# Two more tile pairs of block 0 by Strassen's identity, and statistics by way of DRAM, in a fused LayerNorm, state-space and feed-forward kernel

## The chip, the cores and the metric

One Trainium2 chip, one core. The time is device microseconds of one execution; the kernel before takes 357.88 us, the median of three runs (357.68 to 357.89). The engines are TensorE (PE, with its weight loads as PEld), VectorE (DVE), ScalarE (ACT), GpSimd (POOL) and SyncE (SP, which only issues transfers here).

## The reference

The input is u of [1, 2048, 640]. The output is the sum of three things: u itself, a state-space layer of the normalised u, and a feed-forward layer of the normalised u.

```
xn  = layernorm(u)                      # over the 640 features
K   = 2 Re sum_n C[d,n] exp(dt A[d,n])^l
ssm = causal_conv(xn, K) + xn * D_skip  # over the 2048 positions
h   = xn @ w1 + b1                      # 640 -> 1728
ffn = (h * tanh(softplus(h))) @ w2      # 1728 -> 640
out = u + ssm + ffn
```

## The kernel before, in words

Everything is held transposed, features on partitions: KD = 5 slabs of 128 features, and positions along the rows, in NB = 4 blocks of TB = 512. The hidden size is cut into 14 tiles (FC): tiles 0 to 7 and 9 to 13 have 128 units, tile 8 (HALF) has 64.

The feed-forward products are made in float16. Each operand is split in a high and a low part (xh and xl for x, w1h and w1l, w2h and w2l, hi and lo for the activations), and three products are added in PSUM: high by high, low by high, high by low. A tile of the first layer (mm1, L807) is therefore 5 slabs x 3 = 15 matmuls of 512 columns, and so is a tile of the second layer (mm2_ops, run at L859). The second layer follows LAG = 3 tiles behind.

Two tiles that lie side by side (PAIRS names the first: 0, 2, 4, 6, 9, 11) can be made together by Strassen's identity in Winograd's form (mm1_pair, L809 to L834). Four slabs of x and of w1 and the two halves of the block's positions form 2 x 2 blocks, of which 7 products are needed and not 8; the fifth slab is done plainly. That makes 54 matmuls of 256 columns in five pieces: one (12), two (15), three_a and three_b (9 each) and four (9). In between, ACT copies two partial results out of PSUM (cV and cY, L1049 and L1050) and DVE adds one to another (z, L1053, wanted by three_a; w, L1057, wanted by four). Pieces of second layers stand between the five, so that these steps have time. A pair needs more operands: sums and differences of the block's x (sum_x at L613, their high parts th at L616 and low parts tl at L620), once for a block, and sums of the two weight tiles (sum_w at L580 to L586, their high and low parts at L598 and L602), once for the kernel. In the kernel before, pairs are used in blocks 1 to 3; block 0 makes all its tiles plainly. The sums of the weights are made from tiles that are loaded a second time (load_s, L573).

After a first layer come the activation's steps: ACT's s (L890), DVE's A (L894), three ACT steps p (L898 to L906), DVE's A (L910), then hi (ACT, L916) and lo (DVE, L926).

LayerNorm. Block 0 is normalised in the start-up, position by position. Later blocks load u twice. Untransposed tiles x feed the statistics (st, DVE, L627 to L629; four for a block). POOL turns the variances into factors (rstds, L633, L634, L1213). The means and the factors, 128 x 8, are turned by a PE transpose (spread, L638), copied by ACT (L642), stored to DRAM as 8 rows (sd, L646) and broadcast to all partitions (bc, L650). Transposed slabs xt are loaded, and DVE subtracts the mean and multiplies by the factor (L654, both operations; ten for a block). Then xh and xl are made (L565, L568). 

The state-space layer. Parameters are checked to be so small that the convolution comes to prefix sums within given bounds; the checks and the few constants are DVE and ACT steps on parameter tiles (L671 to L690, and the exponentials at L197 to L212), called the preparation of the parameters below. The sums are the skip steps (L743 to L763). A value per partition, ok, gathers the checks of parameters and weights; a matmul with ones (ok_sum, L731) adds it over the partitions, DVE makes the flag of it, and every engine reads the flag (L734). If it is set, a general path runs behind. In block 0, x is put together again from xh and xl for these steps (x0_sum, L1197).

Joining. A block's second layer is copied out of PSUM (join, L768 on DVE for two slabs, L770 on ACT for three), u is added by a POOL transfer that accumulates (L548), the result is accumulated on the state-space part (L773), and stored.

The order of the work. PE's order is written out in whole(). For ACT, DVE, SP and POOL a planner (class Plan) goes along a model of the time and takes, on each engine, the ready step with the earliest due time; due times are worked out backwards from PE's. An engine then runs its steps in just this order: a step that waits holds up all behind it. So each number of cost, gap or due time moves steps.

## Time and profile before

| | us |
|---|---|
| median of three runs | 357.88 |
| span of the profiled execution | 356.0 |
| PE busy | 350.0 |
| DVE busy | 305.9 |
| ACT busy | 295.8 |
| POOL busy | 48.9 |
| block 0's pairable tiles 9 to 13 begin on PE | 57.9 |
| block 1 begins on PE | 88.8 |
| block 2 begins | 173.4 |
| block 3 begins | 258.0 |

The page's span is the time from the first to the last instruction of one profiled execution; the runs' time is 1.9 us longer than that. Matmuls overlap: a row's duration is longer than the time to the next row's start, and a price on PE is taken from start to start. Names in rows leave out buffer numbers; L859 is line 859 of the kernel before.

### The profile page before, as it was taken

Reading aid. Unit: us, or ns where it says so; the run is one execution under the profiler, and the core shown is the slowest. Engines: PE = TensorE matmul, PEld = TensorE weight load, DVE = VectorE, ACT = ScalarE, POOL = GpSimd, SP = SyncE. Lnnn points to the kernel's source line nnn. Section 1 sums busy time; section 2 is a strip of 40 time slices with the busy share of each in tenths; the row PEclk is TensorE's granted clock in tenths of the full one; section 3 lists DMA queues with packets and bytes.
Section 4 is the critical chain, followed back from the end, with each engine's and each line's share of the span. In section 5 each row is a group of like instructions: output and inputs, shape, how many; then the busy total and the mean of one; then the engine's idle time right before and its main releaser. Section 6 shows DMA issues by size and latency. Waiting matters only on the chain.

```text
span 356.0 us, 6197 instructions
## 1 busy us (share of the span) xinstructions
PE 350.0 (98%) x2257; PEld 215.1 (60%) x2257; DVE 305.9 (86%) x583; ACT 295.8 (83%) x620; POOL 48.9 (14%) x74
## 2 busy tenths in 40 slices
PE   7999999999999999999999999999999999999996
PEld 6754444444666666665566666566566666666543
DVE  5989989989999999999999877899988878895552
ACT  4699999987598699989899977989989979877650
POOL 2200010000014221000004341000002443000000
PEclk9999999999999999999999999999999999999999
DMA  7869964402819926910445982931000994032004
GB/s 266 327 175 288 321 217 121 142 0 66 287 56 159 295 71 142 347 40 3 130 151 88 252 204 77 309 120 40 28 0 7 164 216 102 18 58 32 2 2 152
DMA packets 26052, 48.75 MB, mean 137 GB/s; under 512 B 3592, under 2 KB 6944, under 8 KB 26016
## 3 DMA queue, kind: packets, MB, share of 16 engines
q1 hardware_dynamic: 19488, 34.86, 30.0%
q0 software_dynamic: 6240, 13.11, 18.5%
q8 instruction: 19, 0.31, 0.4%
q10 hardware_dynamic: 288, 0.33, 0.3%
q14 instruction: 17, 0.14, 0.2%
HBM read 39.10 MB, written 5.26 MB: 125 GB/s over the span
## 4 chain that ended last, share of the span: by engine, by line
PE 96%; DVE 1%; DMA 1%; ACT 0%; issue 0%
PE acc L859 48%; PE h L827 18%; PE h L807 12%; PE tr L827 12%; PE h L800 2%; PE h L789 2%; PE tr L789 1%; DMA x<-in_A_u_dram 1%; PE acc L1236 0%; DVE st L627 0%; DVE st L628 0%; ACT x L1224 0%; PE acc L873 0%; PE acc L871 0%; PE acc L870 0%; DVE w1l L556 0%
## 5 line engine op out<-in xcount | busy, mean ns | idle before, releaser
L859 PE MATMUL acc<-hi,w2h 128*128 128x512 f16 x273 | 100.9, 379 | 0.0
L859 PE MATMUL acc<-hi,w2l 128*128 128x512 f16 (+1 forms) x265 | 99.7, 379 | 0.0
L859 PE MATMUL acc<-lo,w2h 128*128 128x512 f16 x253 | 93.3, 379 | 0.0
L859 PEld LDWEIGHTS <-w2h 128*128 128x128 f16 x526 | 50.9, 98 | 48.3 <-issue 2.1
L890 ACT ACTIVATE s<-h,cv 128x512 f32<-128x512 f32 (+1 forms) x55 | 32.7, 595 | 28.6 <-PE h L827 23.4
L827 PEld LDWEIGHTS <-w1h 128*128 128x128 f16 x432 | 42.3, 98 | 10.7
L910 DVE SCALAR_TENSOR_TENSOR A<-p,A 128x512 f32<-128x512 f32 (+1 forms) x56 | 37.1, 662 | 8.5 <-ACT p L906 8.2
L859 PEld LDWEIGHTS <-w2l 128*128 128x128 f16 x273 | 25.6, 98 | 30.7 <-issue 1.1
L926 DVE SCALAR_TENSOR_TENSOR lo<-A,hi 128x512 f16<-128x512 f32 x52 | 35.5, 683 | 8.0 <-ACT hi L916 8.0
L894 DVE SCALAR_TENSOR_TENSOR A<-h,bs,s 128x512 f32<-128x512 f32 (+1 forms) x55 | 34.9, 637 | 6.2 <-ACT s L890 6.2
L898 ACT ACTIVATE p<-s,kc 128x512 f32<-128x512 f32 (+1 forms) x56 | 39.4, 703 | 0.6
L902 ACT ACTIVATE p<-p,kc 128x512 f32<-128x512 f32 (+1 forms) x56 | 39.4, 703 | 0.5
L906 ACT ACTIVATE p<-p,kc 128x512 f32<-128x512 f32 (+1 forms) x56 | 39.3, 702 | 0.4
L916 ACT ACTIVATE hi<-A 128x512 f16<-128x512 f32 x52 | 32.5, 626 | 2.6 <-DVE A L910 2.5
L548 POOL DMA_DIRECT2D r<-in_xT_dram x15 | 13.4, 1003 | 131.7 <-DVE r L768 66.3
L749 DVE TENSOR_TENSOR_SCAN g<-g,car,kc 128x512 f32<-128x512 f32 x20 | 25.6, 1278 | 1.7 <-ACT g L743 1.7
L827 PEld LDWEIGHTS <-w1l 128*128 128x128 f16 x216 | 21.1, 98 | 8.2
L753 DVE TENSOR_TENSOR_SCAN g<-g,car,g 128x512 f32<-128x512 f32 x20 | 25.5, 1276 | 0.0
L827 PE MATMUL tr<-xh,w1l 128*128 128x256 f16 x90 | 24.5, 273 | 0.0
L827 PE MATMUL tr<-xh,w1h 128*128 128x256 f16 x90 | 24.5, 273 | 0.0
L827 PE MATMUL tr<-xl,w1h 128*128 128x256 f16 x90 | 24.5, 273 | 0.0
L827 PEld LDWEIGHTS <-swh 128*128 128x128 f16 x216 | 21.1, 98 | 4.4
(177 smaller groups left out, 726.6 us busy)
## 6 DMA issues: line engine op xcount, KB each, us to landing
w<-in_w_dram SPq DMA_DIRECT2D x25, 320.0 KB, 4.9
x<-in_A_u_dram SPq DMA_DIRECT2D x14, 320.0 KB, 5.0
w<-in_w2T_dram SPq DMA_DIRECT2D x15, 288.0 KB, 6.4
w<-in_B_w_dram SPq DMA_DIRECT2D x13, 320.0 KB, 3.4
w<-in_w1T_dram SPq DMA_DIRECT2D x13, 320.0 KB, 7.0
xt<-in_xT_dram SPq DMA_DIRECT2D x15, 256.0 KB, 5.6
r<-in_xT_dram POOLq DMA_DIRECT2D x15, 256.0 KB, 5.6
xt<-r POOLq DMA_DIRECT2D x15, 256.0 KB, 4.6
```

Of the source, the lines that this page charges most:

```text
L749: v.tensor_tensor_scan(g1[:, 1:], g1[:, 1:], zero.to_broadcast([P, TB]), car[:, 1, k:k + 1], op0=OP.add, op1=OP.add)
L807: pe.matmul(o, w, x, start=(j == 0), stop=(j == len(order) - 1))
L827: pe.matmul(o, p, q, start=start and n == 1, stop=n == 3 * len(w), skip_group_check=True)
L859: pe.matmul(o, w, x, start=start, stop=stop)
L890: a.activation(pl["s", b, f][:, c], bank(b, f)[:, c] if h is None else h, AF.Sigmoid, bias=cv[:, f:f + 1], scale=1 / SH)
L894: v.scalar_tensor_tensor(pl["A", b, f][:, c], bank(b, f)[:, c] if h is None else h, bs[:, f:f + 1], pl["s", b, f][:, c], op0=OP.add, op1=O ...
L898: a.activation(pl["p", b, f][:, cols(f)], pl["s", b, f][:, cols(f)], AF.Arctan, bias=one, scale=-1.0)
L902: a.activation(p, p, AF.Square, bias=pi4, scale=2.0)
L906: a.activation(p, p, AF.Tanh, bias=mb, scale=MG)
L910: v.scalar_tensor_tensor(A, pl["p", b, f][:, cols(f)], MC, A, op0=OP.add, op1=OP.mult)
L916: a.activation(hi, A, AF.Copy, scale=MA * SA / SH)
L926: v.scalar_tensor_tensor(lo, A, MA * SA / SH, hi, op0=OP.mult, op1=OP.subtract)
```

## The change

Five things are changed, and the order of nearly all steps with them.

1. Block 0's tiles 9 and 10, 11 and 12 (EARLY) are made as pairs. For that, block 0's x sums with their high and low parts are made (sums(0, ...)), the x0 sums are made early, and these two pairs' weight sums come from the w1 tiles that lie in SBUF for block 0 anyhow (sum_w with own), so that their second loads go. Tiles 9 to 13 use the PSUM banks in the later blocks' way (bank).
2. The statistics are stored to DRAM straight from the partitions (spread_d: 128 partitions with 8 values each, to a [8, 128] array read as r p -> p r). The PE transpose and ACT's copy go. POOL stores the mean's negative.
3. The mean is no longer subtracted on DVE. Five POOL transfers for a block read the stored row, broadcast it and accumulate it on the loaded slab (center). DVE keeps the multiplication.
4. The flag: ok is stored to DRAM, read back as a row, and DVE takes its minimum; ok_sum's matmul goes.
5. All joins are on ACT. The preparation of the parameters is due in block 1, tile 7, and no longer at block 0's end; costs, gaps and other due times are new, and SHIFT moves single due times by a table of some 270 numbers.

How the order changes at the places that matter. First DVE in block 0, when PE works on tiles 9 and 10. Before, w2l, hi and A belong to the running tiles, par and mx to the preparation of the parameters:

```order
L674 TENSOR_REDUCE mx_463<-par_564 128x10
L926 SCALAR_TENSOR_TENSOR lo3_256<-A1_245,hi3_255 128x512 [waits Activation_49]
L678 SCALAR_TENSOR_TENSOR par_564,sm_464<-par_564,dt_110 128x128 [waits DVE_49]
L910 SCALAR_TENSOR_TENSOR A0_244<-p0_247,A0_244 128x256 [waits Activation_49]
L678 SCALAR_TENSOR_TENSOR par_564,sm_464<-par_564,dt_110 128x128
L580 TENSOR_TENSOR t0_229<-w6_225 128x256 [waits DMAHW7_49]
L678 SCALAR_TENSOR_TENSOR par_564,sm_464<-par_564,dt_110 128x128
L562 SCALAR_TENSOR_TENSOR w2l9_163<-w3_222,w2h9_149 128x640 [waits DMAHW0_49,Activation_49]
L678 SCALAR_TENSOR_TENSOR par_564,sm_464<-par_564,dt_110 128x128
L582 TENSOR_TENSOR t0_229<-t0_229,w1_220 128x256 [waits DMAHW6_49,DVE_49]
```
After, t2 with xt is an x difference, tl and el low parts of such, swl and w1l those of weight sums, st_905 the last of block 1's four statistics, and L1080 the first new pair's z:

```order
L638 SCALAR_TENSOR_TENSOR swl4_196<-t2_229,swh4_190 128x256
L638 SCALAR_TENSOR_TENSOR w1l12_136<-t0_227,w1h12_123 128x2x128 [waits Activation_49]
L649 TENSOR_TENSOR t2_229<-xt_643,t3_230 128x512 [waits DVE_49]
L656 SCALAR_TENSOR_TENSOR el_207<-t1_228,eh_206 128x256 [waits Activation_49]
L945 SCALAR_TENSOR_TENSOR A1_242<-p0_244,A1_242 128x512
L945 SCALAR_TENSOR_TENSOR A0_241<-p1_245,A0_241 128x256 [waits Activation_49]
L656 SCALAR_TENSOR_TENSOR tl3_205<-t2_229,th3_201 128x512 [waits Activation_49]
L961 SCALAR_TENSOR_TENSOR lo3_253<-A1_242,hi3_252 128x512 [waits Activation_49]
L663 BN_STATS st_905<-x1_226 128x6 [waits DMAHW6_49]
L664 BN_STATS st_905<-x1_226 128x6
L665 BN_AGGR mv_570<-st_905 128x2 [waits DVE_49]
L1080 TENSOR_TENSOR h0_209<-h1_210,pvs_211 128x256 [waits PE_49]
```
The preparation of the parameters is gone from here, sums and their low parts have come, and the statistics have moved back from far ahead to right before z.

Second DVE some 10 us later, where block 1 is normalised. Before, L654 is the subtraction (bc0) and the multiplication (bc1), among steps of the parameters:

```order
L654 TENSOR_TENSOR xt_575<-xt_575,bc0_240 128x512 [waits DMAHW1_49]
L910 SCALAR_TENSOR_TENSOR A2_246<-p1_248,A2_246 128x512 [waits DVE_49,Activation_49]
L678 SCALAR_TENSOR_TENSOR par_564,sm_464<-par_564,dt_110 128x128
L654 TENSOR_TENSOR xt_575<-xt_575,bc0_240 128x512
L678 SCALAR_TENSOR_TENSOR par_564,sm_464<-par_564,dt_110 128x128
L654 TENSOR_TENSOR xt_575<-xt_575,bc0_240 128x512
L926 SCALAR_TENSOR_TENSOR lo1_252<-A2_246,hi1_251 128x512 [waits PE_49,Activation_49]
L681 TENSOR_TENSOR mx_463<-mx_463 128x5
L654 TENSOR_TENSOR xt_575<-xt_575,bc0_240 128x512
L894 SCALAR_TENSOR_TENSOR A1_245<-h1_212,bs_104,s0_242 128x512 [waits Activation_49]
```
After, L1080 and L1084 are z and w of the second new pair, and L684 is the multiplication, which waits for the accumulating transfer of the mean (a DMASW semaphore):

```order
L945 SCALAR_TENSOR_TENSOR A1_242<-p1_245,A1_242 128x512 [waits Activation_49]
L1080 TENSOR_TENSOR h0_209<-h1_210,pvs_211 128x256 [waits PE_49]
L684 TENSOR_TENSOR xt_576<-xt_576,bc0_238 128x512 [waits DMAHW3_49,DMASW0_49]
L929 SCALAR_TENSOR_TENSOR A0_241<-tr_208,bs_102,s1_240 128x256 [waits Activation_49]
L961 SCALAR_TENSOR_TENSOR lo2_251<-A1_242,hi2_250 128x512 [waits Activation_49]
L1084 TENSOR_TENSOR h1_210<-h1_210,pvs_211 128x256 [waits PE_49]
L684 TENSOR_TENSOR xt_576<-xt_576,bc0_238 128x512 [waits DMASW1_49]
L596 SCALAR_TENSOR_TENSOR w2l12_164<-w6_223,w2h12_150 128x640 [waits DMAHW6_49,Activation_49]
L929 SCALAR_TENSOR_TENSOR A0_241<-h0_209,bs_102,s1_240 128x256 [waits Activation_49]
```
The multiplications now stand between z and w.

Third SP, on the statistics' way. Before, sr is ACT's copy of the transposed statistics, and two broadcasts follow the store at once:

```order
L573 DMA w1_220<-in_w1_dram 128x640 [waits DMAHW6_49,DVE_49]
L573 DMA w6_225<-in_w1_dram 128x640 [waits DMAHW7_49,DVE_49]
L646 DMA sd_861<-sr_858 8x128 [waits DMAHW0_49,Activation_49]
L650 DMA bc0_240<-sd_861 128x512 [waits DMAHW1_49,DMAHW0_49]
L650 DMA bc1_241<-sd_861 128x512 [waits DMAHW2_49]
L573 DMA w3_222<-in_w1_dram 128x640 [waits DMAHW3_49,DVE_49]
```
After, the store takes st_row from the partitions, and three loads stand between it and the one broadcast:

```order
L573 DMA w6_223<-in_B_w2_dram 128x640 [waits DMAHW6_49,DMAHW0_49,DVE_49]
L674 DMA sd_956<-st_row_571 128x8x1 [waits Pool_49]
L607 DMA w4_221<-in_w1_dram 128x640 [waits DVE_49]
L607 DMA w1_218<-in_w1_dram 128x640 [waits DMAHW1_49,DVE_49]
L573 DMA w3_220<-in_B_w2_dram 128x640 [waits DMAHW2_49,DVE_49]
L677 DMA bc0_238<-sd_956 128x512 [waits DMAHW7_49,DMAHW3_49]
```
The five transfers that take off the mean stand on POOL, right behind the steps that make the factors:

```order
L669 TENSOR_SCALAR st_row_571<-mv_570 128x4 [waits DVE_49]
L670 TENSOR_TENSOR st_row_571<-st_row_571,kc_89 128x4 [waits Pool_49]
L1250 TENSOR_SCALAR st_row_571<-mv_570 128x4
L680 DMA xt_576<-sd_956 128x512 [waits DMAHW7_49,DMAHW6_49]
L680 DMA xt_576<-sd_956 128x512 [waits DMAHW4_49]
```
The way of the statistics now has no step on PE and ACT, one broadcast on SP less, and five transfers on POOL that were not there.

The core of the diff, where SHIFT's table and the moved calls of the planner are left out:

```diff
+EARLY = (9, 11)
...
-    GAP = {"PE": 0.22, "ACT": 0.12, "DVE": 0.12, "SP": 0.0, "POOL": 0.3}
+    GAP = {"PE": 0.17, "ACT": 0.14, "DVE": 0.12, "SP": 0.0, "POOL": 0.3}
...
+        ops = list(self.ops.values())
+        for i, x in SHIFT:
+            for u in ("due", "soft"):
+                ops[int(i)][u] += float(x)
...
-    pl.pool("b", [[row.tile([P, TB], F32, name=f"bc{j}") for j in range(2)]])
+    pl.pool("b", tiles(row, "bc", 1, [P, TB]))
...
+    def first_k(f):
+
+        return 1 if f - 1 in EARLY else 0
...
-        w = lambda n, m: kf(pl["sw", i, n])[:, 0:4].rearrange("p (q j) f -> p q j f", j=2)[:, :, m]
+        own = PAIRS[i] in EARLY
+        w = lambda n, m: kf(pl["w1", PAIRS[i] + n] if own else pl["sw", i, n])[:, 0:4].rearrange(
+            "p (q j) f -> p q j f", j=2)[:, :, m]
...
-        a.activation(EH if j == 4 else TH[j], stage(c, j), AF.Copy, scale=SX)
+        a.activation(EH if j == 4 else TH[j], stage(c, j), AF.Copy, scale=SX if c else 1.0)
...
-    def spread():
-
-        pe.transpose(TR[:2 * NT, 0:P], NX["st"].rearrange("p j i -> p (j i)"), ident)
-
-    def spread_a():
-        NX["sr"] = tmp.tile([2 * NT, P], F32, name="sr")
-        a.copy(NX["sr"], TR[:2 * NT, 0:P])
-
     def spread_d():
         NX["sd"] = dram.tile([2 * NT, P], F32, name="sd")
-        sp.dma_start(NX["sd"], NX["sr"])
+        sp.dma_start(NX["sd"].rearrange("r p -> p r"), NX["st"].rearrange("p j i -> p (j i)"))
 
     def spread_l(c):
-        for j in range(2):
-            sp.dma_start(pl["b", c][j], NX["sd"][j * NT:(j + 1) * NT].rearrange("(o i) p -> o (i p)", o=1).to_broadcast([P, TB]))
-
-    def norm_t(c, k, j):
+        sp.dma_start(pl["b", c], NX["sd"][NT:2 * NT].rearrange("(o i) p -> o (i p)", o=1).to_broadcast([P, TB]))
+
+    def center(c, k):
+        g.dma_start(XT[c][:, k], NX["sd"][0:NT].rearrange("(o i) p -> o (i p)", o=1).to_broadcast([P, TB]), accum_op=OP.add)
+
+    def norm_t(c, k):
         z = XT[c][:, k]
-        v.tensor_tensor(z, z, pl["b", c][j], op=(OP.subtract, OP.mult)[j])
+        v.tensor_tensor(z, z, pl["b", c], op=OP.mult)
...
-    def ok_sum():
-        pe.matmul(TR[:, 0:1], ones, SM["ok"], start=True, stop=True)
+    def ok_row():
+        NX["ok"] = tmp.tile([1, P], F32, name="ok_row")
+        z = dram.tile([P], F32, name="ok_dram", bufs=1)
+        sp.dma_start(z.rearrange("(p o) -> p o", o=1), SM["ok"])
+        NX["okd"] = z
+
+    def ok_back():
+        sp.dma_start(NX["ok"], NX["okd"].rearrange("(o p) -> o p", o=1))
...
-        v.tensor_scalar(flag, TR[0:1, 0:1], P - 0.5, None, op0=OP.is_lt)
+        z = tmp.tile([1, 1], F32, name="ok_all")
+        yield lambda: v.tensor_reduce(z, NX["ok"], axis=AX.X, op=OP.min)
+        yield lambda: v.tensor_scalar(flag, z, 0.5, None, op0=OP.is_lt)
...
-        if k < 2:
-            v.tensor_scalar(r, ACC[k], 1 / SO, None, op0=OP.mult)
-        else:
-            a.activation(r, ACC[k], AF.Copy, scale=1 / SO)
+        a.activation(r, ACC[k], AF.Copy, scale=1 / SO)
...
+        if b > 0 or f >= EARLY[0]:
...
+        paired = lambda b, f: f in (PAIRS if b else EARLY)
...
+        for k in range(KD):
+            add(("x0s", k), V, 0.602, x0_sum, k, pre=[("x0s", 0)] * (k > 0), rel=start(0, 5))
+        sums(0, lambda ks: [("x0s", k) for k in ks], lambda j: [])
...
-            add(("rs", c), G, 2.6, rstds, pre=[("st", c, NT - 1)])
-            add(("sr", c), A, 0.25, spread_a, pre=[("spread", c)])
-            add(("sd", c), S, 0.1, spread_d, pre=[("sr", c)], kb=4.0)
-            add(("bc", c), S, 0.2, spread_l, c, pre=[("sd", c)], take=("b", ("b", c), 2 * KD), kb=512.0)
+                add(("st", c, i), V, 1.04, stats, c, i, pre=[("lx", c, i)] + [("st", c, i - 1)] * (i > 0), drop=[("x", c, i)])
+            add(("rs", c), G, 2.0, rstds, pre=[("st", c, NT - 1)])
+            add(("sd", c), S, 0.1, spread_d, pre=[("rs", c)], kb=200.0)
+            add(("bc", c), S, 0.2, spread_l, c, pre=[("sd", c)], take=("b", ("b", c), KD), kb=256.0)
...
-                add(("n", c, k, 0), V, 0.62, norm_t, c, k, 0, pre=[("lxt", c), ("bc", c)], drop=[("b", c)])
-                add(("n", c, k, 1), V, 0.62, norm_t, c, k, 1, pre=[("n", c, k, 0)], drop=[("b", c)])
+                add(("n", c, k, 0), G, 1.0, center, c, k, pre=[("lxt", c), ("sd", c)], kb=512.0)
+                add(("n", c, k, 1), V, 0.602, norm_t, c, k, pre=[("n", c, k, 0), ("bc", c)], drop=[("b", c)])
...
+        line = [i for i, f in enumerate(PAIRS) if f in EARLY] + [i for i, f in enumerate(PAIRS) if f not in EARLY]
+        for o, i in enumerate(line):
+            f = PAIRS[i]
+            both = [("w1", f), ("w1", f + 1)] if f in EARLY else [("sw", i, 0), ("sw", i, 1)]
...
-                due=start(0, 13))
+                due=start(1,7))
...
+        add(("okd",), S, 0.1, ok_row, pre=last, kb=1.0)
+        add(("okr",), S, 0.1, ok_back, pre=[("okd",)], kb=1.0)
+        fns = list(ok_end())
+        add(("oke", 0), V, 0.2, fns[0], pre=[("okr",)])
+        add(("oke",), V, 0.17, fns[1], pre=[("oke", 0)])
...
-        g.tensor_copy(NX["st"][:, 0], NX["mv"][:, :, 0])
+        g.tensor_scalar(NX["st"][:, 0], NX["mv"][:, :, 0], -1.0, None, op0=OP.mult)
```

166 lines of the change are left out of this document (77 added, 89 removed), and 21 rows, old and new, of the table SHIFT.

## The prediction

> **What bounds the kernel now.** I read the page's busy times first, then TensorE's waits, then busy time by stage, then the rows of single steps. The page says that TensorE (PE) is busy nearly all the time.
>
> ```profile
> span 356.0 us, 6197 instructions
> PE 350.0 (98%) x2257; PEld 215.1 (60%) x2257; DVE 305.9 (86%) x583; ACT 295.8 (83%) x620; POOL 48.9 (14%) x74
> ```
>
> A busy share alone can hide slow steps, so I looked at what PE waited for. The whole list has two entries, both in the start-up, before the first feed-forward products:
>
> ```profile
> PE tr L1246 <- POOL ident masks.py:199: 1.5, 1, 1.5
> PE acc L1236 <- ACT x L1224: 1.0, 1, 1.0
> ```
>
> So from block 0's first products to the end the time is the sum of PE's steps. A PE step taken out shortens the run by its start-to-start time, unless a new wait appears. The stages show who could bring one. The columns are stretch, length, PE, PEld, DVE, ACT, POOL busy, granted clock, DMA share and GB/s.
>
> ```profile
> 17.00:88.80 71.80, 71.80 (x372) 34.34 (x370) 67.01 (x153) 66.69 (x119) 1.43 (x3) 1.00 0.53 164
> 88.80:173.40 84.60, 84.60 (x576) 54.45 (x575) 81.88 (x155) 74.03 (x163) 14.17 (x18) 1.00 0.56 155
> 17.00:57.90 40.90, 40.90 (x228) 20.63 (x226) 37.35 (x78) 40.84 (x75) 1.43 (x3) 1.00 0.77 238
> 57.90:61.20 3.30, 3.30 (x17) 1.46 (x15) 3.05 (x13) 2.67 (x9) 0.00 (x0) 1.00 0.03 11
> ```
>
> The first row is block 0, the second block 1. The clock is full. In block 0 DVE has 71.80 - 67.01 = 4.8 us free and ACT 5.1, and up to 57.9 us ACT is never idle. The change puts new work into just this stretch.
>
> **What PE saves.** The second column is the duration, and starts tell the price:
>
> ```profile
> 82.36 1.24 PE L807 MATMUL h<-xh,w1h 128*128 128x512 f16 x5
> 85.60 0.38 PE L859 MATMUL acc<-hi,w2h 128*128 128x512 f16 x1
> 88.84 0.27 PE L827 MATMUL tr<-th,w1h 128*128 128x256 f16 x1
> 90.15 0.38 PE L859 MATMUL acc<-hi,w2h 128*128 128x512 f16 x1
> 49.31 0.27 PE L638 MATMUL tr<-ident,st_row 128*8 128x128 f32 x1
> 49.42 0.38 PE L859 MATMUL acc<-hi,w2h 128*128 128x512 f16 x1
> 321.43 0.28 PE L731 MATMUL tr<-ok,ones 128*128 128x1 f32 x2
> 321.57 0.38 PE L859 MATMUL acc<-hi,w2h 128*128 128x512 f16 x1
> ```
>
> A plain tile has 15 matmuls of 512 columns, 85.60 - 82.36 = 3.24 us (0.216 each). The 12 of a pair's first part take 90.15 - 88.84 = 1.31, 0.109 each, so a pair's 54 take 5.89 where two plain tiles take 6.48. Two pairs save 2 x 0.59 = 1.18 us. The three transposes cost 0.11 each by the next start, the flag's matmul 0.14: 0.47. Together 1.65 us, and with no new wait 357.88 - 1.65 = 356.2 us. (The span is 1.9 us below the median of the runs; I take what lies around it as unchanged and set the difference against the median.)
>
> The Trainium skill, "TensorE: Matmul & The Clock Gate", Part 4 (PE-mode transpose), gives a transpose about 275 ns inside a kernel. The trace agrees as to the duration (0.27), but PE starts the next step after 0.11; by the page's figure the three would be worth 0.83 us and the sum without a wait would be 355.7.
>
> **What DVE gets, and by when.** Rows of one kind give the prices (count, busy, mean ns):
>
> ```profile
> L613 DVE TENSOR_TENSOR t<-xt 128x512 f32<-128x512 f32 x6 | 4.1, 683 | 0.0
> L620 DVE SCALAR_TENSOR_TENSOR tl<-t,th 128x512 f16<-128x512 f32 x12 | 8.2, 680 | 0.6 <-ACT th L616 0.6
> L1197 DVE TENSOR_TENSOR xt<-xh,xl 128x512 f32<-128x512 f16 x5 | 3.4, 683 | 0.0
> L582 DVE TENSOR_TENSOR t<-t,w 128x256 f32<-128x256 f32 x6 | 2.5, 419 | 0.0
> L674 DVE TENSOR_REDUCE mx<-par 128x10 f32<-128x1280 f32 x1 | 1.5, 1477 | 0.0
> L678 DVE SCALAR_TENSOR_TENSOR par<-par,dt 128x128 f32<-128x128 f32 x10 | 3.5, 348 | 0.0
> L205 DVE TENSOR_TENSOR exp_p<-exp_p,exp_t 128x5 f32<-128x5 f32 x4 | 0.7, 166 | 0.1
> L654 DVE TENSOR_TENSOR xt<-xt,bc 128x512 f32<-128x512 f32 x30 | 20.0, 683 | 0.0
> 57.92 3.24 PE h L807 x15
> ```
>
> Over the whole kernel DVE loses 15 subtractions (L654, 10.2 us) and some joins, and gains about 8 us of sums; ACT gains six to seven. Blocks 1 to 3 have room for that (block 1: ACT 10.6 us free), and there the removed subtractions help. Block 0 decides.
>
> The last row is tile 9's start in the chain, where the first new pair will stand. Its DVE step z must end before PE's third part: 57.92 + 12 x 0.109 + 9 x 0.216 + 15 x 0.109 + 9 x 0.216 = 64.7. In the new order there stand on DVE ahead of that z, beyond what it had begun by 61.2 before: five x0 sums (L1197, 3.4), five x differences and five low parts (four full, one half of 0.42: 3.15 + 3.14), four weight sums of 0.42 (1.7) and their low parts (1.9). Gone from there are the preparation of the parameters (the reduce 1.48, four L678 1.4, twenty small ones at 0.166 3.3) and 1.3 of other rows. Net +5.8 us. With z itself (0.43) that is 6.3 us, of which 3.5 fit between 61.2 and 64.7. The other 2.8 must come out of DVE's idle time, which was 44.20 - 37.35 - 3.05 = 3.8 us from 17 to 61.2. PE therefore doesn't wait only if DVE's idle falls from 3.8 to about 1.0. Back-to-back steps start some 0.08 us before the former ends, so 1.1 is nearer.
>
> How much will be left? The first and the last of the four early waits, and the only later one of size, are
>
> ```profile
> 17.71 0.75 DVE L894 SCALAR_TENSOR_TENSOR A<-h,bs,s 128x512 f32<-128x512 f32 x1 [0.45 <-ACT s L890]
> 22.61 0.82 DVE L562 SCALAR_TENSOR_TENSOR w2l<-w,w2h 128x640 f16<-128x640 f32 x1 [0.43 <-ACT w2h L559]
> 46.14 0.75 DVE L894 SCALAR_TENSOR_TENSOR A<-h,bs,s 128x512 f32<-128x512 f32 x1 [0.83 <-ACT s L890]
> ```
>
> The four come to 1.7 us by 22.6, all on ACT, before any new DVE work is at hand (one low part of tile 5 moves up among them). The 0.83 should go, since DVE will by then run behind ACT. I take 1.7 us, hence a stall of 1.7 - 1.1 = 0.6 us at z or at ACT's copy before it: ACT gets 0.6 us more by then and had 3.30 - 2.67 = 0.6 idle in the last stretch, so it is no slacker. Bounds: nothing, if the early waits shrink below 1.1, and 2.7, if DVE loses its 3.8 as before. The second pair has nearly the same margin and doesn't add to this; a stall moves both.
>
> **The statistics' new way.** The last statistics rows now stand just ahead of that z, some 20 us later than before. What follows is priced by
>
> ```profile
> 44.15 0.25 POOL L633 TENSOR_SCALAR st_row<-mv 128x4 f32<-128x4 f32 x1 [31.30 <-DVE exp_t L201]
> 45.48 0.19 POOL L1213 COPY st_row<-mv 128x4 f32<-128x4 f32 x1
> 56.62 0.35 SPq L646 DMA_DIRECT2D sd<-sr  x1
> 60.04 0.82 SPq L650 DMA_DIRECT2D bc<-sd  x2
> L773 POOL DMA_DIRECT2D xt<-r x15: 850/872/909, 111.7 to 287.6; - x15
> DMA to landing us min/median/max: 3.2/4.6/8.3
> q1 hardware_dynamic: 19488, 34.86, 30.0%
> w<-in_w_dram SPq DMA_DIRECT2D x25, 320.0 KB, 4.9
> 314.18 0.15 DVE L728 TENSOR_TENSOR ok<-ok,z 128x1 f32<-128x1 f32 x1
> 320.96 0.41 DVE L1057 TENSOR_TENSOR h<-h,pvs 128x256 f32<-128x256 f32 x1
> L734 PEldq TENSOR_LOAD <-flag x1: 487/487/487, 330.7 to 330.7; - x1
> ```
>
> POOL needs 45.67 - 44.15 = 1.5 us; the statistics' store held the broadcast back 60.04 - 56.62 = 3.4; the first accumulating DMA, like those of L773, 0.87 on POOL and 4.6 to land. From z's 64.2: 64.2 + 1.5 + 3.4 + 0.9 + 4.6 = 74.6. The first multiply that needs it stands on DVE right behind the second pair's z, and behind it are queued a product A, a low part, and the second pair's w, for which PE waits before its last part. PE reaches that part at 57.92 + (5.89 + 30 x 0.216) + 1.31 + 1.93 + 1.64 + 5 x 0.216 + 1.96 + 4 x 0.216 = 79.1; the four rows (0.68, 0.47, 0.68, 0.43) must begin by 76.8. So 2.2 us are spare, and I price this at nothing. But the store now has 1024 elements of 4 bytes apart where it had 8 rows. A queue-1 packet took 0.30 x 16 x 356 / 19488 = 0.088 us; were each element one, 1024 over 16 engines would be 5.6 us more: PE would stall 3.4. The Trainium skill, "DMA: Bandwidth & Descriptors", Rules for kernel authors, says that a strided last dimension lowers to one descriptor per element; no run here shows such a store yet. In the other two blocks DVE's margin is over 10 us by the same count, which covers either price.
>
> Queues: on SP the store waits for POOL (65.7), and behind it stand two loads for weight sums, a second-layer weight and the broadcast of the factors. Those loads wait for buffers that DVE frees a few rows behind z, at about 67.5, ahead of the store's landing (69.1); with 4.9 us they land by 73, and DVE takes that weight only behind w. On POOL the five accumulating DMAs stand ahead of loads for joins of block 1. All that at nothing; without the cover, the multiply is late as above. The flag: ok is ready at 314.3, PE reads the flag at 330.7; two small DMAs at 3.4 end by 321.2, and DVE's reduce stands behind the fifth pair's w, which began at 320.96 before. If the DMAs take 2 us longer, DVE loses those at a place where it is often idle: nothing.
>
> **Rivals.**
> 1. No stall at all: 356.2. For it: PE's list of waits has no entry past the start-up. Against: 1.7 us of early idle on DVE.
> 2. Slower: DVE keeps losing 3.8 us to ACT in block 0. z ends 2.7 us late: 356.2 + 2.7 = 358.9, 1.0 above before. It decides from an idle of 2.8 us on (stall 1.7, gain gone). For it: ACT is full to 57.9 and gets more; against: most of what DVE waited for were results that it had caught up with, and now it lags.
> 3. The store of single elements lands late. From 3.4 + 2.2 = 5.6 us on PE waits behind the multiply; with 6.2 to 9.0 us the time is 356.8 to 359.6.
> 4. The saving is no saving, because a 256-column step in block 0 is dearer than in block 1: same time as before, 357.9. The equal clock in both rows speaks against it.
>
> **How the numbers follow.** Likeliest: 356.2 + 0.6 = **356.8 us**, with 356.4 to 357.3 around it (0.50). Rival 1 0.16, rival 2 0.16, rival 3 0.13, rival 4 0.05. A measurement can tell 0.2%, 0.7 us, so faster means under 357.2, slower over 358.6. Faster: most of the forecast's own (0.44) and rival 1: 0.60. Same: the rest of the forecast, rival 4 and half of rival 3: 0.17. Slower: 0.23. The range goes from 356.1 to 359.2; left out are the upper end of rival 3, worse stalls and a larger saving.
>
> **What would show it.** Right: PE's list of waits names DVE's or ACT's steps of block 0's two pairs with 0.3 to 1.1 us in all, block 1's first pair starts 0.2 to 1.0 us earlier than 88.84 (1.18 + 0.11 less the stall), and stages 1 to 3 keep their lengths less 0.11 (0.14) for the transposes. Rival 2 shows as a wait over 1.5 us at the first pair's third part with DVE idle over 2.8 us before it; rival 3 as DVE idle ahead of the multiply with the accumulating DMA as what ended it, and PE waiting for w. Wrong altogether: a PE wait in blocks 1 to 3, or a start-up that is longer by more than 0.3 us.

## The result, and the profile after

The changed kernel takes **390.01 us**, the median of five runs (389.57 to 391.46); the kernel before took 357.89 beside it (357.68 to 358.12). The ratio is 1.0905, with a 95% interval of 1.089 to 1.092. The forecast was 356.8 with a range up to 359.2: it was wrong by far, and in the sign.

The page of the changed kernel (span, busy times, granted clock in 40 slices, and packets):

```profile
span 388.2 us, 6310 instructions
PE 355.9 (92%) x2300; PEld 222.5 (57%) x2300; DVE 300.7 (77%) x579; ACT 301.4 (78%) x634; POOL 63.0 (16%) x88
PEclk9999999969999999995999998799999999999999
DMA packets 30424, 50.61 MB, mean 130 GB/s; under 512 B 6962, under 2 KB 10291, under 8 KB 30387
```

The span is 32.2 us longer. TensorE (PE) idles 388.2 - 355.9 = 32.3 us where it idled 6.0: 26.3 more. It is also busy 5.9 us longer, although work for 1.65 us was taken out: the granted clock falls in four of the 40 slices, at three places. The waits of PE past the start-up, largest first (total, times, longest):

```profile
PE tr L862 <- ACT h L1077: 15.5, 3, 8.5
PE h L862 <- DVE h L1080: 5.3, 1, 5.3
PE h L862 <- DVE h L1084: 3.3, 2, 2.4
PE tr L862 <- DVE tl L656: 0.9, 1, 0.9
```

They lie at pairs: in block 0 at z (L1080, 5.3 us) and w (L1084, 0.9 us), and for the most part in blocks 1 and 2, at the copy of ACT out of PSUM (L1077). The list of before had nothing after the start-up.

**Block 0.** PE's timeline at the second new pair (start, duration, operation, and in brackets what ended the idle time before it):

```profile
76.67 0.38 PE L894 MATMUL acc<-lo,w2h 128*128 128x512 f16 x1
82.36 0.37 PE L862 MATMUL h<-th,swh 128*128 128x256 f16 x1 [5.31 <-DVE h L1080]
82.52 0.42 PE L862 MATMUL h<-th,swl 128*128 128x256 f16 x1
82.74 0.42 PE L862 MATMUL h<-tl,swh 128*128 128x256 f16 x1
```

PE waits 5.31 us for the second pair's z. VectorE (DVE), which makes z, was not busy; it waited itself:

```profile
75.34 0.41 DVE L638 SCALAR_TENSOR_TENSOR swl<-t,swh 128x256 f16<-128x256 f32 x1
80.94 0.43 DVE L616 TENSOR_TENSOR t<-w 128x256 f32<-128x256 f32 x1 [5.19 <-DMA w<-in_w_dram]
81.28 0.68 DVE L945 SCALAR_TENSOR_TENSOR A<-p,A 128x512 f32<-128x512 f32 x1
81.88 0.42 DVE L1080 TENSOR_TENSOR h<-h,pvs 128x256 f32<-128x256 f32 x1
86.29 0.69 DVE L684 TENSOR_TENSOR xt<-xt,bc 128x512 f32<-128x512 f32 x1 [3.99 <-DMA xt<-sd]
```

The first of these waits is not for the statistics. It is for a weight load of a later pair's weight sum, which stands on DVE ahead of z. SP issued that pair's two loads from 68.0 us on, right behind the store; the second, issued at 68.7, landed at 80.9. The second wait is the one of rival 3: the multiplication (L684) waits for the accumulating transfer, and here it costs PE 0.9 us at w. The next fence has the lines of the trace for the store (L674), for the loads of weight sums (L607), and for the accumulating transfers (L680), each with its time from issue to landing:

```profile
L674 SPq DMA_DIRECT2D sd<-st_row x3: 377/382/383, 66.7 to 214.6; - x3
DMA to landing us min/median/max: 9.6/11.4/12.3
L607 SPq DMA_DIRECT2D w<-in_w_dram x8: 327/352/1002, 56.5 to 79.1; - x8
DMA to landing us min/median/max: 3.4/10.8/12.2
L680 POOL DMA_DIRECT2D xt<-sd x15: 857/876/1557, 77.0 to 245.6; - x15
DMA to landing us min/median/max: 6.2/7.4/12.4
```

The store of 4 KB takes 9.6 to 12.3 us. The loads behind it, which carry ordinary 2560-byte rows, take up to 12.2 as well. The same loads in before (L573 there):

```profile
DMA to landing us min/median/max: 2.8/3.0/7.2
```

The stretch behind the store shows it directly. The columns are those of the prediction; the last three are granted clock, DMA share and GB/s. The share adds up how long packets took, over 16 engines; packets can overlap, so it can pass 1:

```profile
69.00:75.00 6.00, 6.00 (x44) 3.69 (x42) 6.00 (x13) 5.78 (x12) 0.00 (x0) 1.00 0.84 30
```

By the record the DMA engines are 84% busy, and they move 30 GB/s.

**Block 1.** POOL issues the transfers that take off the mean:

```profile
164.88 2.66 POOL L680 DMA_DIRECT2D xt<-sd  x3 [9.11 <-DMA sd<-st_row]
173.72 0.88 POOL L680 DMA_DIRECT2D xt<-sd  x1 [6.17 <-issue]
175.93 0.86 POOL L680 DMA_DIRECT2D xt<-sd  x1 [0.77 <-issue]
```

It waits 9.11 us for the store, issues three, and can issue the fourth only 6.17 us later. From there the delay runs down a line of engines that each wait in order, and ends at the copy that PE needs. DVE first (its first two multiplications; the second is the one that ACT waits for), then ACT (the row that waits and the copy), then PE, in rows of their timelines:

```profile
173.43 0.69 DVE L684 TENSOR_TENSOR xt<-xt,bc 128x512 f32<-128x512 f32 x1 [6.17 <-DMA xt<-sd]
175.65 0.69 DVE L684 TENSOR_TENSOR xt<-xt,bc 128x512 f32<-128x512 f32 x1 [1.53 <-DMA xt<-sd]
```
```profile
176.37 0.63 ACT L599 ACTIVATE xh<-xt 128x512 f16<-128x512 f32 x1 [8.28 <-DVE xt L684]
180.94 0.37 ACT L1077 COPY h<-tr 128x256 f32<-128x256 f32 x1
```
```profile
181.36 0.37 PE L862 MATMUL tr<-xh,w1h 128*128 128x256 f16 x1 [8.46 <-ACT h L1077]
```

The copy needs nothing of the mean. It stands on ACT behind the xh step that does, and ACT had idled 8.28 us. Four stretches show the clock (the column ahead of the DMA share): during that wait, two that begin with its end, and a later one:

```profile
172.00:181.40 9.40, 0.94 (x7) 0.25 (x6) 6.33 (x10) 4.99 (x10) 3.20 (x4) 0.69 1.09 278
181.36:185.74 4.38, 4.38 (x18) 2.60 (x18) 3.19 (x6) 3.48 (x7) 0.57 (x1) 0.50 0.21 63
181.40:187.00 5.60, 5.60 (x28) 3.47 (x28) 4.38 (x7) 4.64 (x10) 0.57 (x1) 0.61 0.19 59
187.00:200.00 13.00, 13.00 (x79) 7.44 (x77) 12.14 (x22) 12.22 (x27) 1.43 (x2) 1.00 0.17 42
```

After the wait the granted clock is 0.50 for 4.4 us, and the matmuls of 256 columns start 0.21 us apart (181.52, 181.74, 181.95) where they took 0.109; the 0.61 is the mean of a stretch that ends at full clock. So each long wait is paid a second time. The Trainium skill, "TensorE: Matmul & The Clock Gate", Part 1 (The HAM clock gate), says that the array falls to half its clock after an idle window of about 3.4 us; the trace agrees, with 0.50 after 8.46 us of waiting.

**Block 2.** The 5.8 us that PE waits there for the same copy come another way. ACT stands for 8.65 us at a check of the weights (L736), ahead of the copy, for a load that SP issued at 228.2:

```profile
236.91 0.74 ACT L736 ACTIVATE w<-w 128x640 f32<-128x640 f32 x1 [8.65 <-DMA w<-in_w1T_dram]
```

### The profile page after: what moved, and what is told of

Its sections match the earlier page's. It is cut to its first block, busy times and chain, and to the rows that moved or that the text cites. A ratio compares the mean times of both kernels' runs of the same rounds, so it can differ in the third digit from the quotient of the medians.

```text
span 388.2 us, 6310 instructions
## 1 busy us (share of the span) xinstructions
PE 355.9 (92%) x2300; PEld 222.5 (57%) x2300; DVE 300.7 (77%) x579; ACT 301.4 (78%) x634; POOL 63.0 (16%) x88
## 2 busy tenths in 40 slices
DMA packets 30424, 50.61 MB, mean 130 GB/s; under 512 B 6962, under 2 KB 10291, under 8 KB 30387
## 4 chain that ended last, share of the span: by engine, by line
PE 58%; DMA 17%; ACT 10%; DVE 9%; issue 3%; POOL 2%; SPq 0%; POOLq 0%; DVEq 0%
PE acc L894 29%; PE h L862 15%; PE tr L862 9%; DMA sd<-st_row 6%; DMA xt<-sd 4%; DMA w<-in_w_dram 3%; PE h L842 3%; DMA w<-in_w1T_dram 2%; ACT s L925 1%; DVE w2l L596 1%; ACT p L933 1%; DVE A L945 1%; ACT p L937 1%; ACT p L941 1%; DMA w<-in_B_w_dram 1%
## 5 line engine op out<-in xcount | busy, mean ns | idle before, releaser
L862 PEld LDWEIGHTS <-w1h 128*128 128x128 f16 x480 | 47.7, 99 | 14.9 <-issue 2.8
L925 ACT ACTIVATE s<-h,cv 128x512 f32<-128x512 f32 (+1 forms) x55 | 32.1, 584 | 21.7 <-PE h L862 19.7
L862 PE MATMUL tr<-xh,w1h 128*128 128x256 f16 x100 | 28.1, 281 | 15.5 <-ACT h L1077 15.5
L862 PEld LDWEIGHTS <-w1l 128*128 128x128 f16 x240 | 23.8, 99 | 28.7 <-issue 20.3
L951 ACT ACTIVATE hi<-A 128x512 f16<-128x512 f32 x52 | 32.2, 624 | 5.5 <-DVE A L945 5.5
L862 PE MATMUL tr<-xl,w1h 128*128 128x256 f16 x100 | 28.1, 281 | 0.1
L862 PE MATMUL tr<-xh,w1l 128*128 128x256 f16 x100 | 28.1, 281 | 0.0
L862 PE MATMUL h<-th,swh 128*128 128x256 f16 x80 | 22.6, 283 | 5.3 <-DVE h L1080 5.3
L862 PEld LDWEIGHTS <-swh 128*128 128x128 f16 x240 | 24.2, 101 | 5.7
```

Source lines behind the costliest of these rows:

```text
L862: pe.matmul(o, p, q, start=start and n == 1, stop=n == 3 * len(w), skip_group_check=True)
L925: a.activation(pl["s", b, f][:, c], bank(b, f)[:, c] if h is None else h, AF.Sigmoid, bias=cv[:, f:f + 1], scale=1 / SH)
L951: a.activation(hi, A, AF.Copy, scale=MA * SA / SH)
```

## The experiments

My first theory was that of rival 3, larger: the chain from store over accumulating transfer to multiplication is longer than the planned order allows for, and only those that wait for the chain lose. Its rival was that pairs and accumulating transfers overfill the engines, whatever the store does. Neither held as it was put.

**1. The store alone, with every step in its place.** rows_same_order stores the same tile as 128 rows of 32 bytes, which puts the values elsewhere. The broadcasts read as many values as before, as they now lie, and the factors are made with exponent 0: the kernel leaves out the true means and factors, and keeps every size. The order on PE, DVE, ACT and POOL is the changed kernel's to the row. The edit of the store:

```
-        NX["sd"] = dram.tile([2 * NT, P], F32, name="sd")
-        sp.dma_start(NX["sd"].rearrange("r p -> p r"), NX["st"].rearrange("p j i -> p (j i)"))
+        NX["sd"] = dram.tile([P, 2 * NT], F32, name="sd")
+        sp.dma_start(NX["sd"], NX["st"].rearrange("p j i -> p (j i)"))
```

> The changed kernel with every instruction in its place; only the statistics' store differs: 128 rows of 32 bytes, one behind the other in DRAM, and not 1024 single values turned round. (What lies in the broadcast row is then not the means and factors, and the factors are computed with exponent 0; the computation is wrong there, the sizes and the order are the same.) Theory 1 (the store's late landing): it lands in about 3 us, the waits of 5.3 us at the second pair's w in block 0, of 8.5 in front of block 1's last pair and most of block 2's go; what the accumulating transfers cost stays, some 2 to 5 us at block 1's first pair: 358 to 364. Theory 2 (the accumulating transfers): 372 to 386. Theory 3 (pairs and due times overfill the engines): 375 to 388.

Measured: 365.61 us, ratio 1.0205 (1.0188 to 1.0223). Its store's landing, PE's waits, and the stretch that stands above for the changed kernel:

```profile
DMA to landing us min/median/max: 1.4/1.4/2.2
```
```profile
PE tr L862 <- ACT h L1077: 5.6, 3, 3.4
PE tr L862 <- DVE tl L656: 0.7, 1, 0.7
```
```profile
69.00:75.00 6.00, 6.00 (x44) 3.68 (x43) 6.00 (x14) 5.78 (x13) 2.90 (x3) 1.00 0.85 237
```

With the same order 24.4 of the 32.1 us are gone, which is the store's part as Theory 1 put it, though the time is 1.6 us above Theory 1's range. Nearly the same DMA share, 0.85, now moves 237 GB/s instead of 30.

**2. The accumulating transfers, in the same order.** Both kernels cut them to 32 of 128 partitions, one with the store of single values and one with the rows:

```
-        g.dma_start(XT[c][:, k], NX["sd"][0:NT].rearrange("(o i) p -> o (i p)", o=1).to_broadcast([P, TB]), accum_op=OP.add)
+        g.dma_start(XT[c][0:P // 4, k], NX["sd"][0:NT].rearrange("(o i) p -> o (i p)", o=1).to_broadcast([P // 4, TB]), accum_op=OP.add)
```

> Every step of the changed program in its place, the strided store as it is; only the 15 accumulating transfers are cut to a quarter, 32 of the 128 partitions (the mean is then taken off those alone). It leaves the store's late landing and takes away most of the transfers' own time, their pause after three on POOL and their load on the other transfers. Theory 1 (the loss is the length of the chain: store, transfer, multiply): about 24 us of the store's stay and what the transfers add goes, 372 to 384 us, the store still landing after 9 to 13 us. Rival (the transfers cost nothing, all is the store): 388 to 391 us. Rival (the transfers' load makes the store late): under 368 us and the store landing under 6 us.

> As rows_same_order (the store in rows of 32 bytes, values elsewhere), and the accumulating transfers cut to 32 partitions as in small_transfers; every step in its place. Theory 1 (what is left in rows_same_order above 356.2 us is the transfers' own lateness, and 0.6 us of start-up): 356.6 to 358.5 us, no wait of TensorE over 1 us past the start-up. Rival (the pairs of block 0 or the order itself cost what is left): 364 to 366 us, with the waits at the same places as in rows_same_order.

| median, us | store of single values | store in rows |
|---|---|---|
| transfers of 128 partitions | 390.0 | 365.6 |
| transfers of 32 partitions | 388.0 | 358.5 |

The intervals of the ratios are 1.079 to 1.092 (388.0) and 1.0003 to 1.0027 (358.5). The store costs 24.4 or 29.5 us. Cutting the transfers wins 7.1 us beside the store in rows, and 2.0 beside the store of single values, which is within the spread of small_transfers' own runs (385.8 to 390.0); that the transfers wait for the store there anyway would explain it, but isn't shown. The first theory's 372 to 384 for small_transfers was missed, and its 356.6 to 358.5 for small_both only just met. With both out of the way, this order, with the pairs of block 0, the joins and the flag as the change has them, runs in 358.5. PE's waits there past the start-up:

```profile
PE tr L862 <- ACT h L1077: 1.7, 3, 1.1
```

So 7.1 us of what rows_same_order left open are the transfers. What is left is 2.3 us above the 356.2 that the prediction has without any wait. These waits are 1.7 us in the profiled run, which took 359.05; runs of this kernel lie between 357.9 and 359.95.

**3. Is it the chain, or the DMA engines?** Each kernel stores the statistics once more behind the broadcast, as 1024 single values, into an array that nobody reads. No step of PE, ACT, DVE or POOL waits for it, and the order of everything else stays. In the kernel before:

```
             sp.dma_start(pl["b", c][j], NX["sd"][j * NT:(j + 1) * NT].rearrange("(o i) p -> o (i p)", o=1).to_broadcast([P, TB]))
+        z = dram.tile([2 * NT, P], F32, name="unread"); sp.dma_start(z.rearrange("r p -> p r"), NX["st"].rearrange("p j i -> p (j i)"))
```

> The kernel before with every step in its place, and for each block one DMA more on SP, behind the two broadcasts: the statistics stored once more, as 1024 single values, into an array that nobody reads. No step waits for it. Theory A (the single values keep the DMA engines from other transfers for some 8 us): loads that are issued behind it land after 8 to 12 us where they took 3 to 5, and the time rises to 361 to 375 us. Theory B (only the store's own landing is late, and the chain store, transfer, multiply waits for it): 357.9 us within 0.5, landing of other loads as before.

> rows_same_order (the store in rows of 32 bytes, which landed after 1.4 us) with the same unread store of 1024 single values behind the broadcast; every other step in its place, none waits for it. The accumulating transfers are in flight beside it. Theory A (the DMA engines are held): 375 to 392 us, most of the 24 us that the rows had won are lost again, and the accumulating transfers land after 12 us or more. Theory B (only the chain's own latency): 365 to 367 us.

Measured: unread_before 364.84 us, ratio 1.019 (1.015 to 1.023), where the kernel before is 357.9; unread_rows 378.99, ratio 1.058 (1.056 to 1.060), where rows_same_order is 365.61. An unread store costs 7.0 and 13.4 us. Three stretches: behind the unread store in unread_before; the same stretch in before; and the one behind it in unread_rows:

```profile
66.00:72.00 6.00, 6.00 (x30) 2.72 (x28) 6.00 (x17) 5.90 (x11) 0.00 (x0) 1.00 0.75 41
```
```profile
66.00:72.00 6.00, 6.00 (x29) 2.70 (x28) 6.00 (x17) 5.87 (x10) 0.00 (x0) 1.00 0.21 69
```
```profile
75.00:81.00 6.00, 4.44 (x31) 2.81 (x29) 1.43 (x4) 2.23 (x5) 0.00 (x0) 1.00 1.35 87
```

In unread_before the DMA engines are 75% busy with 41 GB/s, where 21% sufficed for 69. Rows_same_order moves 310 GB/s in the stretch in which unread_rows moves 87. There PE, DVE and ACT run dry, though none of them waits for the store. SP does, at places that the edit was not meant to have: it takes eight semaphores in turn, and the eighth transfer behind an unread store waits until that store has landed. SP's waits for it, two in unread_before and one in unread_rows:

```profile
SPq L697 <- DMA unread<-st_row: 3.2, 1, 3.2
SPq L700 <- DMA unread<-st_row: 3.1, 1, 3.1
SPq L730 <- DMA unread<-st_row: 5.0, 1, 5.0
```

PE's large waits don't come from there. The two of unread_before (1.3 us at 152.15 and 2.8 at 243.65) go back to checks of the weights on ACT that wait for loads issued within 1.0 us behind the store, ahead of SP's wait; these loads landed after 11.1 and 11.5 us. The two largest of unread_rows (5.4 us at 84.92 and 7.7 at 174.31) are over before SP's only wait ends at 231.7. So what loses the time is that transfers under way land late, the accumulating ones (9.9 us in the median, up to 16.0, in unread_rows; Theory A had expected 12 or more) like the weight loads. This shows the cause: a store of single values keeps the DMA engines from moving other transfers until it lands, some 8 us after its packets have started. A store that is only such a load costs 13.4 us beside rows_same_order, where the true one costs 24.4. The other 11.0 may be the chain's own wait for the store; the split is not sharper than that, because the unread store is issued 2 to 8 us later than the true one and meets other transfers.

**4. POOL's pause after three transfers.** POOL could issue the fourth accumulating transfer only after some 5 to 7 us. Two kernels double the space for its descriptors, nothing else:

```
-_BACC = {"dynamic_dma_scratch_size": 1024}
+_BACC = {"dynamic_dma_scratch_size": 2048}
```

> The run of the same order with rows of 32 bytes and, besides, twice the scratch space for POOL's transfers (2048 where it was 1024), every instruction in its place. It tells what POOL's pause behind three accumulating transfers (6.7 us before the fourth) costs. If the pause is the space for their descriptors: the fourth and fifth are issued without it, and the waits at block 1's first pair go: 1 to 4 us less than with rows alone. If the pause has another reason: the same time as with rows alone.

> The changed kernel as it is, with twice the scratch space for POOL's transfers alone. Theory 1: the store still lands 9 to 12 us after its issue; at most 4 us are won: 384 to 390. Theory 2: most of the loss goes: 357 to 366.

Measured: with the rows 368.5 us, ratio 1.029 (1.023 to 1.036); with the store of single values 395.1, ratio 1.104 (1.102 to 1.106). POOL's timeline and the transfers' landing with the rows:

```profile
69.39 4.69 POOL L680 DMA_DIRECT2D xt<-sd  x5 [3.28 <-DMA sd<-st_row]
```
```profile
DMA to landing us min/median/max: 6.8/10.0/14.3
```

The pause is gone, and nothing is won: five that run together land after 10.0 us in the median, where three at a time took 7.4. So the pause is a matter of the descriptors' space. Both expectations of a gain were missed, and with the store of single values the time even rose, from 390.0 to 395.1. That the transfers' own rate is the limit behind the pause fits these landings and was not taken apart.

**5. Parts taken back, with the order changed by it.** Four kernels undo or do one part. before_direct_store is the kernel before with the strided store in place of transpose and copy. turn_back puts transpose, copy and a store of 8 rows back into the changed kernel; mean_on_dve the second broadcast and the subtraction on DVE; pairs_alone both.

```
-        sp.dma_start(NX["sd"], NX["sr"])
+        sp.dma_start(NX["sd"].rearrange("r p -> p r"), NX["st"].rearrange("p j i -> p (j i)"))
```
```
+    def spread_a():
+        NX["sr"] = tmp.tile([2 * NT, P], F32, name="sr")
+        a.copy(NX["sr"], TR[:2 * NT, 0:P])
...
+        sp.dma_start(NX["sd"], NX["sr"])
```
```
-        g.dma_start(XT[c][:, k], NX["sd"][0:NT].rearrange("(o i) p -> o (i p)", o=1).to_broadcast([P, TB]), accum_op=OP.add)
+        z = XT[c][:, k]
+        v.tensor_tensor(z, z, pl["b", c][0], op=OP.add)
```

> The kernel before with one part of the change alone: the statistics are stored straight from the partitions, without PE's transposes and ACT's copies; the mean stays on DVE, no pairs in block 0. Theory 1: the store lands 9 to 12 us after its issue here too, where it took about 2.5 before, and with due times that reckon with 3 us at least one block's multiplication comes late: 360 to 376. Theories 2 and 3: 357 to 358.5, no wait of PE past the start-up.

> The changed kernel with PE's transpose and ACT's copy of the statistics put back, so that the store to DRAM has 8 rows of 512 bytes again; the mean is still taken off by accumulating transfers, and block 0's two pairs stay. Theory 1 (the store of single 4-byte values, which landed 9.6 to 12.3 us after its issue, is what PE's waits come from): the store lands within 3.5 us, PE's waits past the start-up fall from 25 us to under 5, time 356 to 362 us. Theory 2 (the accumulating transfers, 7.4 us to land and held back on POOL, are the cause): most of the loss stays, 370 to 388. Theory 3 (the pairs and new due times overfill DVE and ACT): 375 to 390.

> The changed kernel with the mean taken off on DVE again (two broadcasts on SP, fifteen subtractions on DVE, no accumulating transfers of the mean); the direct store of single values stays. Theory 1: the store still lands 9 to 12 us late and the broadcasts behind it, so the time stays high, 368 to 390. Theory 2: PE's waits go, 356 to 363. Theory 3: 375 to 392, worse than the changed kernel by DVE's ten microseconds at most.

> The changed kernel with both parts of the statistics' way put back (PE transpose, subtraction on DVE); block 0's two pairs, the flag by way of DRAM, the joins on ACT and the new due times stay. Theories 1 and 2: PE saves 1.18 us by the pairs and 0.14 by the flag and loses 0.6 in the start-up, waits under 2 us: 356.5 to 359.5. Theory 3: over 365, with PE waiting in the two pairs of block 0.

Measured: before_direct_store 376.9 us, ratio 1.053 (1.051 to 1.055); turn_back 383.8, 1.075 (1.070 to 1.080); mean_on_dve 399.0, 1.115 (1.112 to 1.117); pairs_alone 391.6, 1.096 (1.092 to 1.099). The first agrees with what precedes, 0.9 us above the first theory's range: the store, with the order that the planner makes for it, costs the kernel before 19.0 us, with no pair in block 0 and no accumulating transfer. The other three missed the first theory's ranges, and mean_on_dve lies above all three; taken alone, turn_back and pairs_alone would speak for the third theory. But they decide nothing about their parts. The table SHIFT addresses steps by number and was made for the changed program; with other steps and costs the planner makes another order, and small_both, in the changed kernel's own order, runs the same pairs in 358.5. One row of PE's waits in mean_on_dve shows how poor such an order can be:

```profile
PE acc L896 <- DVE w2l L596: 23.5, 1, 23.5
```

A weight's low part, which needs nothing of the mean, comes 23.5 us late.

**6. Orders made for the true landings.** Here the planner is told the measured landing times and the three transfers in flight, and the table is searched anew for each program. In all of them the high part of tile 5's weights is not due before 18 us. honest_due_times keeps the store of single values; pairs_refit is pairs_alone with its own table; the square kernels turn the statistics on DVE in blocks of 32 x 32 and store rows of 128 bytes.

```
+LATE = {'sd': 11.5, 'n': 8.0, 'bc': 7.0}
+RING = 3
...
-                    wait = 4.0 if q["kb"] else self.GAP[q["eng"]]
+                    wait = LATE.get(q["name"][0], 4.0) if q["kb"] else self.GAP[q["eng"]]
```
```
-        sp.dma_start(NX["sd"].rearrange("r p -> p r"), NX["st"].rearrange("p j i -> p (j i)"))
+        for q in range(P // 32):
+            sp.dma_start(NX["sd"][:, q * 32:(q + 1) * 32], NX["sq"][q * 32:q * 32 + 2 * NT])
...
+        v.transpose(NX["sq"], NX["st"].rearrange("p j i -> p (j i)"))
```

> The changed program with all five changes and the same store of single values; only the planner differs: it is told that the store lands after 11.5 us, an accumulating transfer after 8.0, a broadcast after 7.0, and that three POOL transfers are in flight at most; the table of due times is searched anew for these, and the high part of tile 5's weights is not due before 18 us. Theory 1 (the 32 us are the latency of store and transfers that the planned order did not allow for; the work itself fits): 356.5 to 361 us, TensorE's waits past the start-up under 4 us in all, the store still landing after 9 to 13 us. Theory 2 (pairs and accumulating transfers overfill an engine or the transfers, whatever the order): over 365 us, with waits of several us at other places.

> The pairs of block 0 without the statistics' new way: transpose on TensorE, ACT's copy, store of 8 rows and the subtraction on DVE are put back, with a table searched for this program (its plan still has about 2.5 us of waits). Theory 1 (pairs_alone lost 34 us because its table was made for another program): 357.5 to 362 us. Theory 2 (DVE and ACT are too full for the pairs in block 0 with the subtraction on DVE): over 365 us, TensorE waiting for DVE's or ACT's steps in block 0.

> As honest_due_times, but the statistics are turned in blocks of 32 x 32 on DVE (one step more for a block, its cost on DVE taken as about 0.2 us) and stored as 32 rows of 128 bytes by four small transfers; the planner is told 4.5 us for the store, and has its own table. Theory 1: 355.9 to 358.5 us: 356.2 without waits, plus what is left of waits; the stores land within 5 us. Theory 2: over 365 us.

> The same program as square_a with another table, which was chosen to give way less when transfers land late. Theory 1: 355.9 to 358.5 us, within 1 us of square_a. Theory 2: over 365 us.

> The program of square_a; the planner is told 8 us for the flag's store and 3 for its way back as well, and the table is searched anew for orders that hold when single loads land up to 4 us late. Theory 1 (the changed program's work fits once no store of 1024 single values holds the transfers and the order knows the landings): 356.3 to 358.5 us, no wait of TensorE for the flag, waits past the start-up under 2 us in all. Theory 2 (the accumulating transfers load the DMA engines so that some weight load is always late): 360 to 364 us as in square_a and square_b, with a wait of 2 to 4 us that a load ends.

> The same program as square_c with another table from another start, which gave up a little of the plan to be steadier. Theory 1: 356.3 to 358.8 us. Theory 2: 360 to 364 us.

| kernel | us | ratio, 95% interval |
|---|---|---|
| honest_due_times | 377.0 | 1.051 to 1.058 |
| pairs_refit | 372.7 | 1.041 to 1.044 |
| square_a | 363.4 | 1.012 to 1.017 |
| square_b | 361.8 | 1.007 to 1.012 |
| square_c | 360.2 | 1.0045 to 1.0071 |
| square_d | 359.8 | 1.0025 to 1.0054 |

honest_due_times speaks against the first theory as it was put: an order that allows for the store's 11.5 us still loses 19. It is no clean test of the latency alone, since one of its stores landed only after 17.3 us. Without that store the loss falls to 0.4 to 1.5%, but none of the orders beats the kernel before. square_a and square_b lie between the ranges of their two theories; square_c and square_d came out above what Theory 1 expected, square_c in Theory 2's range and square_d just under it. pairs_refit came out as its Theory 2 said, over 365, but does not settle the pairs' own price: 3.3 us of its PE waits are a start-up step, and 5.1 us (1.85 at 327.13, 3.24 at 330.97) stand right behind the place where DVE waits 7.17 us for the flag's way through DRAM.

What is left in square_c is a late load again, at the same place as above:

```profile
77.73 0.43 DVE L684 TENSOR_TENSOR t<-w,w 128x256 f32<-128x256 f32 x1 [1.64 <-DMA w<-in_w_dram]
```

Why such a load now hurts is read from block 0's second part, in the kernel before and in small_both, each from tile 9 (in before the chain's 57.92, its first matmul starts at 57.76) to block 1:

```profile
57.92:88.84 30.92, 30.92 (x147) 13.71 (x145) 29.68 (x76) 25.87 (x46) 0.00 (x0) 1.00 0.22 66
```
```profile
57.67:87.79 30.12, 30.08 (x195) 18.51 (x194) 29.93 (x61) 29.43 (x65) 5.88 (x8) 1.00 0.58 168
```

DVE has 0.2 us free of 30.12, ACT 0.7; before they had 1.2 and 5.1. The transfers move 168 GB/s where they moved 66. So the change took the slack from both engines in the stretch where it also makes loads late. That this is why no order of mine won is argued from these rows, not shown: a better order may exist.

## Why the prediction was wrong

**PE's saving: right.** In small_both the parts of the two new pairs (tiles 9 to 12) take 11.80 us from start to start, against 4 x 3.24 = 12.96: 1.16 saved, 1.18 predicted. In the changed kernel, too, the second new pair begins 12.37 us after the first (70.92 and 58.55), which is 5.89 + 30 x 0.216. Rival 4 falls.

**The stall of 0.6 us at the first new pair's z: did not come.** That pair's parts follow one another without a wait, and the second begins on the predicted distance. Rival 2 falls with it. In small_both DVE had 1.7 us free from 17 to 57.9, just what the working took, but z ended at 64.2, 0.3 us ahead of PE's part (64.50), where the working had it end at 65.3: the new work of DVE was over-counted by about 1 us. The starting point was also 0.16 us late: 57.92 is the start of the chain's piece, and tile 9's first matmul starts at 57.76.

**The statistics' way, priced at nothing: the step that failed.** Three things in it were wrong. First the store: I took 3.4 us, with a bound of 3.4 + 5.6 = 9.0 from the mean time of a packet. It landed after 9.6 to 12.3. The bound scaled by a number of packets, and their time isn't the cost: of the first store's 4-byte packets nearly all start within 2 us and take 9 ns each in the record, and the landing comes some 8 us later. What takes long in the record meanwhile are the packets of the loads, up to 7.4 us for one of 2560 bytes. Rival 3 had the mechanism's first half, at a chance of 0.13 and with a ceiling of 359.6; the wait that it describes cost PE 0.9 us in block 0, and the larger one there, 5.3, is not in it.

Second, and larger, the sentence on SP's queue: "ahead of the store's landing (69.1); with 4.9 us they land by 73". I asked who stands behind the store on SP, but only as to when they are issued. They are issued in time (68.0 to 69.4), and land at 79.3 to 81.7 because the store holds the engines that move them. A transfer was treated as a delay on its own path, not as a load on a resource that all share. This is what unread_before and unread_rows show.

Third, "in the other two blocks DVE's margin is over 10 us": no row of the working gives that margin, and block 1's row leaves DVE 84.60 - 81.88 = 2.7 us. The wait there is one of latency in a fixed order. In block 1's last pair it is store 12.3, three transfers, pause, multiplication, xh on ACT, then a copy that only stands behind them: 8.5 us of PE's waits. In block 2 the same copy stands behind a check whose load lands late: 5.8 us. With 1.2 us at block 1's first pair that makes the 15.5. Average slack doesn't help an engine whose next step in order is not ready.

**The accumulating transfers: under-priced.** I took 4.6 us from transfers that read SBUF; these landed after 7.4 in the median (4.6 to 11.8 even with the quick store). They also come three at a time, which the timeline of before shows at 105.11 us (three issues in a row, then a pause); the working didn't use it. Cutting them to a quarter wins 7.1 us in rows_same_order.

**Not in the sum at all:** the clock after a wait. After its three longest waits PE worked 4.4, 4.4 and 3.1 us at a granted clock of 0.50, 11.9 us in all; half of that, 5.9 us, is what its busy time rose by. With the 26.3 us of added waits these are the 32.2 of the span. **Start-up:** the new order puts the high part of tile 5's weights ahead of xh on ACT, where it waits for its load; xh's last steps began at 15.07 (before 14.14), and at 14.16 to 14.67 in the same order in small_both and rows_same_order. That is 0 to 0.9 us by the load's landing, and I had priced the order of the start-up at nothing.

**The flag at nothing:** this held in the changed kernel, where its store landed after 7.9 us and DVE waited 4.4 at a harmless place. In square_a it stood right ahead of a pair's w (L1136), as that kernel's DVE timeline shows:

```profile
325.69 0.27 DVE L826 TENSOR_REDUCE ok_all<-ok_row 1x1 f32<-1x128 f32 x1 [4.54 <-DMA ok_row<-ok_dram]
325.89 0.41 DVE L1136 TENSOR_TENSOR h<-h,pvs 128x256 f32<-128x256 f32 x1
```

There PE waited 2.7 us for that w: the flag's cover was a matter of place.

The Trainium skill, "DMA: Bandwidth & Descriptors", Rules for kernel authors, says of a strided last dimension that it lowers to one descriptor per element, and advises to rearrange. The trace agrees: packets under 512 bytes rose from 3592 to 6962, about 3 x 1024 and the flag's. The rule spoke against this change, and I gave it too little weight because I turned it into packet time.

**What stays open:** why such packets hold the engines. Not the small size alone, since 128 rows of 32 bytes landed after 1.4 us, and not the count alone, since the flag's 128 single values took 7.9. Nor do the store's own packets fill the engines' time in the record. What the two slow stores have in common is values of 4 bytes that lie next to each other in DRAM and come from different partitions; no run took that apart.
